# Twelve tiles of the last layer's first product as six pairs of seven quarter products, with sums on POOL

## The chip, the cores and the metric

The kernel runs on one core of one Trainium2 chip. The metric is the device time of one execution in microseconds (us); lower is better. Engines are named as the profile names them: PE (TensorE matmul), PEld (its weight load), DVE (VectorE), ACT (ScalarE), POOL (GpSimd), SP (SyncE, whose queue issues most DMAs).

## What is computed

Four residual layers over one sequence of S = 2048 tokens with D = 640 channels: twice (spectral filter, then token-mixing MLP). Cut to what matters here:

```python
def _B_ref(x, w1, b1, w2, b2):
    h = _layernorm(x, axis=-1)                  # (B, S, D)
    u = jnp.einsum("bsd,sf->bdf", h, w1) + b1   # (B, D, F), F = 1728
    u = _gelu(u)                                # tanh form
    y = jnp.einsum("bdf,fs->bds", u, w2) + b2
    return transpose(y)                         # (B, S, D)

x = x + _A_ref(_layernorm(x), A_w_r, A_w_i)     # 2-D FFT, filter, inverse FFT
x = x + _B_ref(_layernorm(x), ...)
x = x + _A_ref(_layernorm(x), ...)
x = x + _B_ref(_layernorm(x), ...)              # the last layer
```

Weights are float32. To keep that precision, the kernel splits each matmul operand into a float16 high part and a float16 low part and adds three products: high·high, high·low, low·high.

## The kernel before

The program is one class with a method for each stage. `run` (line 1411) does the opening stage, then for each of two rounds `a1` (428, filter), `a2` (696, inverse transform, residual and layernorm into `hf`), and the MLP: `b1st` (864) in the first round, `b2nd` (1112) in the second. The change is in `b2nd`, with small parts in `setup`, `a1` and `a2`. Nearly all instructions go through one helper (line 59, `Pin`), so the profile's line says little, and groups are told apart by tile names. While `self.pin` is set, each engine issues its instructions in the order in which the program text makes them.

**First product of the last layer, before.** The 1728 rows of w1's output are 14 tiles of 128 (the last tile holds 64 rows twice, with high parts in one half and low parts in the other; `dup`). The contraction over 2048 tokens is 16 slices j. `h` is kept as `hh[j]` (high) and `hl[j]` (low), each 128 x 2 x 320 (two halves of the channels); its float32 source `hf[j]` is released once `hl` is formed (pop at 1136). A tile takes 16 slices x 3 products x 2 halves = 96 matmuls of 128 x 128 by 320 columns; the dup tile takes 64. The order of tiles is `SEQ` (line 30): 0, 7, 6, 13, 1, 8, ...: a tile and its partner seven further on. The first two tiles go through `both_high` (1093), which multiplies by `hh` while `hl` is still being formed, and then through `rest`.

For each tile of weights: `wload` (828) brings two raw pieces of 128 x 1024 float32 over SP's queue; `wsplit` (840) has ACT write the scaled high part (`wh`) and DVE write raw·s − high (`wl`). After a tile's matmuls, ACT evicts it twice (value and square), DVE and ACT form the gelu in four steps (`q`, tanh, `f`), and `usplit` (1208) forms the operands of the second product: the quarters B11, B21, B22 and the sums T1 to T4 of quarters (`usums`, 1103, on DVE), each as a high part (ACT) and a low part (DVE).

**Second product, before.** It already takes pairs of output tiles d by seven products of quarters in place of eight: A11·B11, S1·T1, S2·T2, S3·T3, A12·B21, S4·B22, A22·T4, where S are sums of weight quarters formed by DVE (`form`, 1164), split by `hi` (ACT, 1181) and `lo` (DVE, 1188), and evictions add the products together. POOL does nothing in either product of this layer.

Of the kernel before, what the change touches and what calls it, by code (L numbers as in the profile page):

```python
# [29 lines left out]
SEQ = [t + 7 * i for t in (0, 6, 1, 2, 3, 4, 5) for i in range(2)]  # L30
# [36 lines left out]
class Layers:  # L67
# [41 lines left out]
    def setup(self):  # L109
# [17 lines left out]
        self.s2, self.c2 = (base.tile([128, NQ], F32, name=f"{a}p") for a in "sc")  # L127
        self.second, self.nr = False, 3
# [299 lines left out]
    def a1(self, first):  # L428
# [4 lines left out]
        self.hh = {j: ph.tile([128, 2, 320], F16, name=f"hh{j}_{self.n}") for j in HA}  # L433
# [262 lines left out]
    def a2(self, li):  # L696
# [4 lines left out]
        self.wp[1] = self.push("wb", side=self.sp)  # L701
        ph = self.push("hf", side=self.sp)
        self.hf = [ph.tile([128, 2, 320], F32, name=f"hf{j}_{self.n}") for j in range(NJ)]
# [399 lines left out]
    def usums(self, f, fs, *names):  # L1103

        B11, B12, B21, B22 = (f[:, i] for i in range(4))
        T1, T2, T3, T4 = (fs[:, i] for i in range(4))
        q = {"T1": (T1, B12, B11), "T2": (T2, B22, T1), "T3": (T3, B22, B12), "T4": (T4, B21, T2)}
        for n in names:
            a, b, c = q[n]
            self.V.tensor_tensor(a, b, c, op=ALU.subtract)  # L1110

    def b2nd(self, li):
# [6 lines left out]
        V, T = self.V, self.T  # L1119
        mm = self.PE.matmul  # L1120
        ADD, SUB, MUL = ALU.add, ALU.subtract, ALU.mult
        ph = self.push("h", side=self.sq)
        for j in range(NJ):
            if j not in HA:
                self.hh[j] = ph.tile([128, 2, 320], F16, name=f"hh{j}_{self.n}")
                T.activation(self.hh[j], self.hf[j], AF.Copy)
        self.pin = True
        self.wsplit(1, hi=False)
        self.h = []
        for j in range(NJ):  # L1130
            self.h.append((self.hh[j], ph.tile([128, 2, 320], F16, name=f"hl{j}_{self.n}")))
            V.tensor_tensor(self.h[j][1], self.hf[j], self.hh[j], op=SUB)
        V.tensor_tensor(self.s2, self.st[1][:, :NQ], self.st[1][:, NQ:], op=ALU.min)
        V.tensor_tensor(self.c2, self.ct[1][:, :NQ], self.ct[1][:, NQ:], op=ALU.max)
        self.pin = False
        self.pop("hf")
        self.nr = 4
        self.wr[1:] = (self.push(a, side=self.sp) for a in ("wr", "wr2", "wr3"))
        px = self.push("px", side=self.sp)
        pu = self.push("u", side=self.sp)  # L1140

        u = [pu.tile([128, 2, 7, 320], F16, name=f"u{f}_{self.n}") for f in range(7)]
        p = self.push("b1", side=self.sq)
        for m in (2, 3, 4, 5):
            self.wload(m)

        def ahead(m):

            self.wload(m + 4)
            if m + 1 < NFT:  # L1150
                self.wopen(m + 1)


        PQ = ("A11", "B11"), ("S1", "T1"), ("S2", "T2"), ("S3", "T3"), ("A12", "B21"), ("S4", "B22"), ("A22", "T4")
        UB = {a: i for i, a in enumerate(("B11", "B21", "B22", "T1", "T2", "T3", "T4"))}
        ops = [(d, *q) for d in range(NQ) for q in PQ]
        NP = len(ops)
        places = [(px, f"wo{i}") for i in range(3)] + [(q, a) for q in self.wp for a in ("wh", "wl")]
        src, wo = {}, {}

        def raw(d, a):
            return self.wraws[NFT + 2 * d + int(a[1]) - 1][int(a[2]) - 1]

        def form(n):

            if n >= NP:
                return
            d, a, _ = ops[n]
            if a[0] == "A":
                src[n] = raw(d, a)  # L1170
                return
            s = src[n] = self.t(px, [128, 7, 128], F32, a, 1)
            x, y, op = {
                "S1": ((d, "A21"), (d, "A22"), ADD), "S2": (n - 1, (d, "A11"), SUB),
                "S3": ((d, "A11"), (d, "A21"), SUB), "S4": ((d, "A12"), n - 3, SUB),
            }[a]
            x, y = (src[q] if isinstance(q, int) else raw(*q) for q in (x, y))
            V.tensor_tensor(s, x, y, op=op)

        def hi(n):  # L1180
            if n >= NP:
                return
            q, tag = places[n % 7]
            w = self.t(q, [128, NJ, 128], F16, tag, 1).rearrange("p (a b) c -> p a b c", a=2)[:, :, :7]
            wo[n] = w
            T.activation(w[:, 0], src[n], AF.Identity, scale=self.s2[:, ops[n][0]:][:, :1])

        def lo(n):
            if n >= NP:
                return  # L1190
            w = wo[n]
            V.scalar_tensor_tensor(w[:, 1], src[n], self.s2[:, ops[n][0]:][:, :1], w[:, 0], op0=MUL, op1=SUB)

        def prep(m):

            for c in range(2):
                if m + 1 < NFT:
                    self.wsplit(m + 1, (c,))
                yield
# [5 lines left out]
        def uhi(t, i, n, f):  # L1205
            T.activation(u[t][:, 0, i:i + n], f, AF.Identity, scale=self.su)

        def usplit(t, k, f, fs):
            if not k:
                uhi(t, 0, 1, f[:, 0:1])  # L1210
                ulo(t, 0, 1, f[:, 0:1])
                self.usums(f, fs, "T1")
                uhi(t, 3, 1, fs[:, 0:1])
                ulo(t, 3, 1, fs[:, 0:1])
            else:
                uhi(t, 1, 2, f[:, 2:])
                self.usums(f, fs, "T2", "T3", "T4")
                ulo(t, 1, 2, f[:, 2:])
                uhi(t, 4, 3, fs[:, 1:])
                ulo(t, 4, 3, fs[:, 1:])  # L1220

        def prod(ps, w, j, h, start=False, stop=False):
            for a in range(2):
                mm(ps[:, a, :320], w[:, j], h[:, a], start=start, stop=stop)

        dup = lambda m: SEQ[m] == NFT - 1

        def rest(m, ps, w):
            for j in range(NJ):
                yield j  # L1230
                prod(ps, w[0], j, self.h[j][1], stop=j == NJ - 1)

        def both(m, ps, w):
            for j in range(NJ):
                yield j
                prod(ps, w[0], j, self.h[j][0], start=j == 0)
                prod(ps, w[0], j, self.h[j][1], stop=dup(m) and j == NJ - 1)
                if not dup(m):
                    prod(ps, w[1], j, self.h[j][0], stop=j == NJ - 1)


        w = self.w.pop(0), self.w.pop(1)
        pss = self.big(), self.big()
        self.both_high(pss, w, prod)
        gc, gs = 1.0 / GC, GS * GC
        later = []
        for m in range(NFT):
            t, k = SEQ[m] % 7, SEQ[m] // 7
            if m < 2:
                ps, run = pss[m], rest(m, pss[m], w[m])  # L1250
                if m:
                    self.wopen(2)
            else:
                ps = self.big()
                run = both(m, ps, self.w.pop(m))
                ahead(m)
            steps = prep(m)
            for j in run:
                if m and j in ((1, 2) if m == 1 else (6, 8) if m == 2 else (2, 4)):
                    next(steps)  # L1260
                if j == 10:
                    for a in later:
                        a()
                    later = []
                if m == NFT - 2 and j == 8:
                    form(1)
                if m == NFT - 1 and j in (1, 4, 7, 10):
                    n = j // 3
                    if n != 1:
                        form(n)  # L1270
                    hi(n)
                    lo(n)
            pv, bb, c1 = ps[:, :, :320], self.b1[:, SEQ[m]:SEQ[m] + 1], self.ct[0][:, SEQ[m]:SEQ[m] + 1]
            if dup(m):

                sw = self.t(p, [128, 2, 320], F32, "sw", 1)
                T.activation(sw[:64], pv[64:], AF.Copy)
                T.activation(sw[64:], pv[:64], AF.Copy)
                V.tensor_tensor(sw, pv, sw, op=ADD)
                pv = sw  # L1280
            if not k:
                f = self.t(p, [128, 4, 320], F32, "f", 2)
                fs = self.t(p, [128, 4, 320], F32, "fs", 1)
            x = f[:, 2 * k:2 * k + 2]
            q = self.t(p, [128, 2, 320], F32, "q", 2)
            if m < NFT - 1:
                T.activation(x, pv, AF.Identity, scale=c1, bias=bb)
# [95 lines left out]
        for n in range(NP + 1):  # L1383
# [11 lines left out]
            if n:  # L1395
                hi(n + 3)
            if n > 1:
                lo(n + 2)
# [303 lines left out]
```

## Time and profile before

| | |
|---|---|
| runs shown | 1030.52 us median of 3 (1027.93 to 1032.33) |
| profiled execution, own time | 1028.95 us |
| its span | 1027.2 us |
| PE / PEld busy | 986.3 / 735.7 us (96% / 72%) |
| DVE / ACT / POOL busy | 725.5 / 571.2 / 265.7 us |
| granted TensorE clock, mean | 0.98 |

The span runs from the first to the last instruction; 1.75 us of the execution lie outside it. Matmuls are pipelined, so one matmul's recorded 299 ns is longer than the distance from one to the next; a few matmul records are missing. "Releaser" is the engine whose event ended a wait. The chain of waits follows the work that ended last, in order of time.

### The profile page before, as it was taken

Reading aid. Unit: us, or ns where it says so; the run is one execution under the profiler, and the core shown is the slowest. Engines: PE = TensorE matmul, PEld = TensorE weight load, DVE = VectorE, ACT = ScalarE, POOL = GpSimd, SP = SyncE. Lnnn points to the kernel's source line nnn. Section 1 sums busy time; section 2 is a strip of 40 time slices with the busy share of each in tenths; the row PEclk is TensorE's granted clock in tenths of the full one; section 3 lists DMA queues with packets and bytes.
Section 4 is the critical chain, followed back from the end, with each engine's and each line's share of the span. In section 5 each row is a group of like instructions: output and inputs, shape, how many; then the busy total and the mean of one; then the engine's idle time right before and its main releaser. Section 6 shows DMA issues by size and latency. Waiting matters only on the chain.

```text
span 1027.2 us, 20943 instructions
## 1 busy us (share of the span) xinstructions
PE 986.3 (96%) x8379; PEld 735.7 (72%) x8379; DVE 725.5 (71%) x1422; ACT 571.2 (56%) x874; POOL 265.7 (26%) x438
## 2 busy tenths in 40 slices
PE   4889999999999999999998999999999999999998
PEld 3768777677777777777776787776777777777776
DVE  7968978954333956666666797897655564988885
ACT  5847768675554556555542575774544454544541
POOL 6927857500000002222222675780000000000000
PEclk9589999999999999999999999999999999999999
DMA  7855356522222264444312644756322232445511
GB/s 230 277 173 168 116 167 222 207 83 99 77 77 74 72 233 155 138 135 123 124 55 86 214 125 130 223 177 210 108 82 83 72 109 77 141 154 175 164 44 52
DMA packets 55738, 139.48 MB, mean 136 GB/s; under 512 B 6461, under 2 KB 12249, under 8 KB 55641
## 3 DMA queue, kind: packets, MB, share of 16 engines
q1 hardware_dynamic: 54200, 131.97, 40.1%
q0 software_dynamic: 1440, 6.17, 2.0%
q8 instruction: 66, 1.08, 0.4%
q14 instruction: 32, 0.25, 0.1%
HBM read 115.05 MB, written 23.07 MB: 134 GB/s over the span
## 4 chain that ended last, share of the span: by engine, by line
PE 76%; DVE 13%; POOL 3%; issue 3%; DMA 2%; ACT 2%; SPq 0%; POOLq 0%; DVEq 0%; ACTq 0%
PE ps L59 76%; DVE st L59 2%; POOL xt L59 2%; DVE xt L59 2%; DVE f L59 1%; DVE Yl L59 1%; DVE s1l L59 1%; DVE hl L59 1%; DVE ta L59 1%; ACT eh L59 1%; DVE el L59 1%; DMA rest<-s1l 1%; POOL r L59 1%; DVE tb L59 1%; DMA stk<-rest 1%
## 5 line engine op out<-in xcount | busy, mean ns | idle before, releaser
L59 PEld LDWEIGHTS <-wh 128*128 128x128 f16 x2992 | 289.7, 98 | 113.4 <-issue 1.8
L59 PEld LDWEIGHTS <-wl 128*128 128x128 f16 x1616 | 157.9, 98 | 62.2 <-DVE wl L59 0.9
L59 PE MATMUL ps<-hh,wh 128*128 128x320 f16 x896 | 186.6, 299 | 0.7 <-ACT hh L59 0.7
L59 PE MATMUL ps<-hl,wh 128*128 128x320 f16 x896 | 184.7, 299 | 0.0
L59 PE MATMUL ps<-hh,wl 128*128 128x320 f16 x832 | 171.4, 299 | 0.6 <-DVE wl L59 0.6
L59 DVE SCALAR_TENSOR_TENSOR wl<-raw,s,wh 128x1024 f16<-128x1024 f32 (+2 forms) x88 | 105.4, 1202 | 87.4 <-ACT wh L59 87.3
L59 PE MATMUL ps<-uh,wl 128*128 128x320 f16 x448 | 133.1, 299 | 0.0
L59 PE MATMUL ps<-ul,wh 128*128 128x320 f16 x448 | 133.1, 299 | 0.0
L59 ACT ACTIVATE wh<-raw,s 128x1024 f16<-128x1024 f32 (+2 forms) x92 | 94.7, 1047 | 68.4 <-PE ps L59 61.6
L59 PE MATMUL ps<-uh,wh 128*128 128x320 f16 x416 | 124.3, 299 | 0.0
L59 ACT ACTIVATE junk<-raw 128x896 bf16<-128x896 f32 (+1 forms) x60 | 59.6, 994 | 46.5 <-DMA raw<-w 46.4
L59 POOL TENSOR_TENSOR r<-v,mh 128x1 f32<-128x1 f32 x64 | 37.4, 584 | 132.2 <-DVE nm L59 122.6
L59 PE MATMUL ps<-tDi,Yh 128*128 128x322 f16 x320 | 71.3, 300 | 0.2
L59 PE MATMUL ps<-u,wo 128*128 128x320 f16 x504 | 69.9, 299 | 0.0
L59 DVE TENSOR_TENSOR f<-eo 128x256 f32<-128x256 f32 (+1 forms) x124 | 39.1, 368 | 38.8 <-POOL eo L59 38.1
L59 PEld LDWEIGHTS <-wo 128*128 128x128 f16 x504 | 49.3, 98 | 19.1
L59 POOL TENSOR_TENSOR xt<-xt,ec 128x320 f32<-128x320 f32 x64 | 52.4, 841 | 32.8 <-DVE xt L59 32.6
L59 PE MATMUL ps<-ph,tS 128*128 128x321 f16 (+2 forms) x288 | 59.6, 289 | 1.3 <-DVE tb L59 1.3
L59 ACT ACTIVATE z<-xt,nb,r 128x640 f32<-128x640 f32 x31 | 28.5, 919 | 55.8 <-POOL z L59 43.5
L59 DVE BATCH_NORM_STATS2 st<-xt 128x6 f32<-128x320 f32 x126 | 55.3, 481 | 5.7 <-DMA xt<-x 4.6
L59 PE MATMUL ps<-tM,f 128*128 128x128 f32 x160 | 39.5, 426 | 19.8 <-DVE f L59 19.8
L59 POOL TENSOR_TENSOR eo<-z 128x320 f32<-128x320 f32 x62 | 53.3, 880 | 17.1 <-ACT z L59 15.1
(174 smaller groups left out, 1877.0 us busy)
## 6 DMA issues: line engine op xcount, KB each, us to landing
raw<-w SPq DMA_DIRECT2D x56, 512.0 KB
xt<-x SPq DMA_DIRECT2D x79, 320.0 KB
w<-w SPq DMA_DIRECT2D x48, 321.0 KB
x<-xt SPq DMA_DIRECT2D x47, 320.0 KB
raw<-w SPq DMA_DIRECT2D x32, 448.0 KB
raw<-w2z SPq DMA_DIRECT2D x32, 448.0 KB
out<-xt SPq DMA_DIRECT2D x15, 320.0 KB
tIM<-tIM POOLq DMA_DIRECT2D x8, 512.0 KB, 5.6
```

Of the source, the lines that this page charges most:

```text
L59: i = f(*a, **k)
```

## The change

The last layer's first product now computes only tiles 6 and 13 whole (`SEQ = [6, 13]`). The other twelve tiles are six pairs (d, d + 7), d = 0 to 5. Each pair is four quarters of weights (two tiles x two halves of the contraction) by four quarters of `h` (two halves of the contraction x two halves of the channels), taken by the same seven products as the second product. A product is 8 slices x 3 matmuls = 24 matmuls of 320 columns, 168 for a pair.

- The sums of weights S1 to S4 (128 x 1024 float32) are formed on POOL, S2, S3, S4 in place of raw quarters. DVE still forms them in the second product, except S1, S2, S3 of its first pair, which POOL forms.
- The sums of h, T1 to T4, are formed on POOL in place in `hf`'s rows (`tsum`: two instructions of 128 x 1280 each), then split by ACT (`thi`) and DVE (`tlo`). So `hf` stays until then, as one tile `hfa`; `hh` for j < 8 becomes one tile `hha`.
- Evictions put the seven products together: ACT and DVE read the product from PSUM, POOL adds pieces already in SBUF. The T sums of `u` (`usum`) move from DVE to POOL, except for the last pair.
- Raw quarters come through a ring of six buffers (`pump`), split weights through five places (`places`).
- At the start, work on tiles 6 and 13 is interleaved with the first sums; the seven products of pairs 0, 1 and 2 are interleaved as `FIRST` says; at the end, the last pair is finished in pieces (`half`, `split1`).

The diff, cut to its core:

```diff
-SEQ = [t + 7 * i for t in (0, 6, 1, 2, 3, 4, 5) for i in range(2)]
+SEQ = [6, 13]
...
-        self.hh = {j: ph.tile([128, 2, 320], F16, name=f"hh{j}_{self.n}") for j in HA}
+        self.hha = ph.tile([128, 8, 2, 320], F16, name=f"hha{self.n}")
+        self.hh = {j: self.hha[:, j] for j in HA}
...
-        self.hf = [ph.tile([128, 2, 320], F32, name=f"hf{j}_{self.n}") for j in range(NJ)]
+        self.hfa = ph.tile([128, NJ, 2, 320], F32, name=f"hf{self.n}")
+        self.hf = [self.hfa[:, j] for j in range(NJ)]
...
+        FIRST = "A11.0 A12.0 S1.0 S2.0 A11.1 A12.1 S3.0 S4.0 A22.0 S1.1 S2.1 A11.2 S3.1 S4.1 A22.1 S1.2 S2.2 A12.2 S3.2 S4.2 A22.2"
+        ops = [(int(q[-1]), q[:-2], P1[q[:-2]]) for q in FIRST.split()]
+        ops += [(d, *q) for d in range(3, ND) for q in P1.items()]
...
+        places = [(self.wp[0], "wl"), (self.wp[1], "wl"), (px, "wo"), (self.wp[0], "wh"), (self.wp[1], "wh")]
...
+        def form(n, W=V, p=None):
...
+            W.tensor_tensor(s, x, y, op=op)
...
+        def tsum(a, c, W=G):
+            j, k = slice(4 * c, 4 * c + 4), slice(8 + 4 * c, 12 + 4 * c)
+            B11, B12, B21, B22 = hfa[:, j, 0], hfa[:, j, 1], hfa[:, k, 0], hfa[:, k, 1]
+            o, x, y = {"T1": (B12, B12, B11), "T2": (B22, B22, B12), "T3": (B11, B22, B11), "T4": (B21, B21, B22)}[a]
+            W.tensor_tensor(o, x, y, op=SUB)
...
+        def tlo(a):
+            for c in range(2):
+                j = slice(4 * c, 4 * c + 4)
+                V.tensor_tensor(TT[a][1][:, j], tsrc(a, c), TT[a][0][:, j], op=SUB)
...
+        def product(n):
...
+            for j in range(8):
+                self.mm3(o, (w[:, 0, j], w[:, 1, j]), operand(b, j), j == 0, j == 7)
...
+            if a == "S2":
+                vs[d] = self.t(p, [128, 320], F32, "v", 1)
+                add(vs[d], ms[d])
+                G.tensor_tensor(f[:, 1], f[:, 1], vs[d], op=ADD)
+            if a == "A12":
+                act(0, bias=b0)
+                G.tensor_tensor(f[:, 0], f[:, 0], ms[d], op=ADD)
+            if a == "S3":
+                add(vs[d], vs[d])
+                (V if end else G).tensor_tensor(f[:, 3], f[:, 3], vs[d], op=ADD)
...
+            elif a == "A22":
+                act(2, bias=b1)
+                G.tensor_tensor(f[:, 2], f[:, 2], vs[d], op=ADD)
...
+        for d in range(3, ND):
+            b = at[d, "A11"]
+            forms.update({(d, "S1"): b - 5, (d, "S3"): b - 3, (d, "S2"): b - 2, (d, "S4"): b + 1})
+        for (d, a), n in sorted(forms.items(), key=lambda q: q[1]):
+            mid[n].append(lam(form, at[d, a], G))
+        for a, n in (("S1", N1 - 4), ("S3", N1 - 3), ("S2", N1 - 2)):
+            mid[n].append(lam(form, at2[0, a], G))
...
+        form(at[0, "S1"], G)
+        hlow(0)
+        hlow(1)
+        hi(0)
+        lo(0)
+        tsum("T1", 0)
+        tsum("T1", 1)
+        hlow(2)
+        hlow(3)
+        hi(1)
+        for i, w in enumerate((wh0, wh1)):
+            prod(pss[i], w, hlows, low)
+        product(0)
+        for i, w in enumerate((wh0, wh1)):
+            prod(pss[i], w, hlows, high, stop=True)
+        thi("T1")
+        hi(2)
+        tlo("T1")
+        lo(2)
+        lo(1)
+        form(at[0, "S3"], G)
+        tsum("T2", 0)
+        tsum("T2", 1)
+        form(at[0, "S2"], G)
...
+        product(1)
...
+        for n in range(2, N1):
+            product(n)
+            for e in first[n]:
+                e()
+            for e in mid[n]:
+                e()
+            hi(n + 3)
+            lo(n + 3)
+            for e in last[n]:
+                e()
+            pump()
```

`first[n]` holds the evictions of product n − 1, `mid[n]` the sums of weights (and T3, T4 at n = 2), `last[n]` the gelu steps and the splits of `u`. `N1` is 42.

More of the change, by code (lines that the diff above doesn't have):

```diff
@@ L127, in setup @@
         self.s2, self.c2 = (base.tile([128, NQ], F32, name=f"{a}p") for a in "sc")
+        self.s1p, self.c1p = (base.tile([128, 7], F32, name=f"{a}p1") for a in "sc")
         self.second, self.nr = False, 3
@@ L1120, in b2nd @@
         mm = self.PE.matmul
         ADD, SUB, MUL = ALU.add, ALU.subtract, ALU.mult
+        self.wr[1] = self.push("wr", side=self.sq)
+        px = self.push("px", side=self.sq)
         ph = self.push("h", side=self.sq)
[L1123 to L1154, printed above, removed]
@@ L1155, in b2nd @@
-        UB = {a: i for i, a in enumerate(("B11", "B21", "B22", "T1", "T2", "T3", "T4"))}
-        ops = [(d, *q) for d in range(NQ) for q in PQ]
-        NP = len(ops)
-        places = [(px, f"wo{i}") for i in range(3)] + [(q, a) for q in self.wp for a in ("wh", "wl")]
+        pt = self.push("T", side=self.sq)
+        hx = self.push("hx", side=self.sq)
+        hha, hfa, hf = self.hha, self.hfa, self.hf
+        hhb, hlb = (ph.tile([128, 8, 2, 320], F16, name=f"{a}b{self.n}") for a in ("hh", "hl"))
@@ new lines, in b2nd, with pump @@
+        order = []
+        for d in range(ND):
+            names = ("A11", "A21", "A12", "A22"), ("A11", "A12", "A21", "A22"), ("A11", "A22", "A21", "A12")
+            order += [(1, d, a) for a in (names[d] if d < 3 else ("A21", "A22", "A11", "A12"))]
+        order += [(2, d, a) for d in range(NQ) for a in ("A21", "A22", "A11", "A12")]
+        pieces, need = {}, {}
+        def pump():
+            while len(pieces) < len(order):
+                k = len(pieces)
+                if k >= 6 and need[order[k - 6]]:
+                    return
+                f, d, a = order[k]
+                r, c = int(a[1]) - 1, int(a[2]) - 1
+                pool, n = (self.wr[0], 2) if k % 6 > 3 else (self.wr[1], 4)
+                raw = self.t(pool, [128, 8, 128], F32, "raw", n)
+                src, q = (A["w1"][d + 7 * r], 8) if f == 1 else (A["w2z"][d + NQ * r], 7)
+                pieces[f, d, a] = raw[:, :q]
+                nc.sync.dma_start(raw[:, :q], src[:, c * q:c * q + q])
+                place = f == 1 or d == 0
+                need[f, d, a] = {
+                    "A11": {"S2"} if place else {"A11", "S2f", "S3f"}, "A21": {"S3"} if place else {"S1f", "S3f"},
+                    "A12": {"S4"} if f == 1 else {"A12", "S4f"}, "A22": {"A22"},
+                }[a]
@@ L1182, in hi @@
                 return
[L1183 to L1186, printed above, removed]
+            if ops[n][1][0] == "A" and n not in src:
+                form(n)
+            q, tag = places[n % 5]
+            w, k = self.t(q, [128, NJ, 128], F16, tag, 1), 8 if n < N1 else 7
+            w = wo[n] = w[:, :2 * k].rearrange("p (a b) c -> p a b c", a=2)
+            T.activation(w[:, 0], src[n], AF.Identity, scale=scale(n))
         def lo(n):
@@ new lines, in hlow @@
+        def hlow(c):
+            j = slice(4 * c % 8, 4 * c % 8 + 4)
+            if c < 2:
+                V.tensor_tensor(hl0[:, j], hfa[:, j, 0], hha[:, j, 0], op=SUB)
+                V.tensor_tensor(hl1[:, j], hfa[:, j, 1], hha[:, j, 1], op=SUB)
+            else:
+                V.tensor_tensor(hlb[:, j], hfa[:, 4 * c:4 * c + 4], hhb[:, j], op=SUB)
+        hhigh = lambda j, a: hha[:, j, a] if j < 8 else hhb[:, j - 8, a]
+        hlows = lambda j, a: (hl1 if a else hl0)[:, j] if j < 8 else hlb[:, j - 8, a]
@@ new lines, in prod, with operand @@
+        def prod(ps, w, h, js, start=False, stop=False):
+            for j in js:
+                for a in range(2):
+                    mm(ps[:, a, :320], w[:, j], h(j, a), start=start and j == 0, stop=stop and j == NJ - 1)
+        def operand(b, j):
+            if b == "B11":
+                return hha[:, j, 0], hl0[:, j]
+            if b[0] == "B":
+                return tuple(q[:, j, int(b[2]) - 1] for q in (hhb, hlb))
+            return tuple(q[:, j] for q in TT[b])
+        bank = {}
@@ L1226, in b2nd @@
[L1226 to L1239, printed above, removed]
@@ L1242, in b2nd @@
-        w = self.w.pop(0), self.w.pop(1)
-        pss = self.big(), self.big()
[L1244 to L1287, printed above, removed]
-                T.activation(q, pv, AF.Square, scale=c1, bias=bb)
-                V.scalar_tensor_tensor(q, q, gc, x, op0=ADD, op1=MUL)
-                T.activation(q, q, AF.Tanh, scale=gs)
-                V.scalar_tensor_tensor(x, q, 1.0, x, op0=ADD, op1=MUL)
-                later.append(lambda t=t, k=k, f=f, fs=fs: usplit(t, k, f, fs))
@@ new lines, in b2nd @@
+        early, late, low, high = range(NJ - 4), range(NJ - 4, NJ), range(8), range(8, NJ)
+        for js in (early, late):
+            prod(pss[0], wh0, hhigh, js, start=True)
+            prod(pss[0], wl0, hhigh, js)
+            prod(pss[1], wh1, hhigh, js, start=True)
+        form(at[0, "S1"], G)
[10 more added lines that the diff above has]
+            prod(pss[i], w, hlows, low)
@@ new lines, in b2nd @@
+        product(0)
[10 more added lines that the diff above has]
+        form(at[0, "S2"], G)
+        self.pop("hx")
+        p = self.push("b1", side=self.sq)
+        pr = self.push("br", side=self.sp)
+        f = pr.tile([128, 4, 320], F32, name=f"fr{self.n}")
+        q0, q1 = (pr.tile([128, 2, 320], F32, name=f"qr{k}{self.n}") for k in range(2))
@@ new lines, in b2nd, with uopen @@
+        last[4] += [g0(1), g0(2), dup1, g0(3), g1(1)]
+        last[5] += [g1(2), lam(thi, "T4"), lam(tlo, "T4"), g1(3)]
+        def uopen():
+            self.pop("br")
+            self.pop("hf")
+            pu = self.push("u", side=self.sp)
+            u.update({t: pu.tile([128, 2, 7, 320], F16, name=f"u{t}_{self.n}") for t in range(7) if t != t0})
+        u = {t0: self.u6}
+        for k in range(3):
+            last[7 + k].append(lambda k=k: usplit(k, t0, f))
+        last[10] = [uopen] + last[10]
@@ new lines, in b2nd, with half, go, split1 @@
+        D5 = ND - 1
+        q5 = {}
+        def half(i, *ks):
+            def go():
+                if i // 2 not in q5:
+                    q5[i // 2] = self.t(p, [128, 2, 320], F32, "q", 2)
+                for k in ks:
+                    gelu(k, fs[D5][:, i:i + 1], q5[i // 2][:, i % 2:i % 2 + 1])
+            return go
+        def split1(i, n, x):
+            return [lambda: uhi(D5, i, n, fs[D5][:, x:x + n]), lambda: ulo(D5, i, n, fs[D5][:, x:x + n])]
+        last[N1 - 3] += [half(0, 0, 1)]
```

247 lines of the change are left out of this document (180 added, 67 removed).

## The prediction

> **What bounds the kernel now.** I read the chain of waits first, then busy times by stretch, then groups by tile and shape, then single instructions in order of time.
>
> ```profile
> 692.29 11.04 DVE hl L59 x15
> ...
> 712.13 311.52 PE ps L59 x2292
> ```
>
> In the chain of waits (start, us, what), from 712 us to the end it is one piece of PE work; just before it DVE forms `hl`. 311.52 / 2292 = 0.1359 us is the distance between matmuls.
>
> ```profile
> 683.18 0.99 PE L59 MATMUL ps<-hh,wh 128*128 128x320 f16 x6
> 695.34 0.43 PE L59 MATMUL ps<-hh,wh 128*128 128x320 f16 x2 [0.19 <-ACT hh L59]
> 863.73 8.31 PE L59 MATMUL ps<-u,wo 128*128 128x320 f16 x60
> ...
> 740.00:760.00 20.00, 20.00 (x150) 14.42 (x148) 9.84 (x14) 7.98 (x10) 0.00 (x0) 1.00 0.29 88
> 875.00:1012.00 137.00, 137.00 (x1011) 98.65 (x1009) 117.26 (x141) 62.75 (x71) 0.00 (x0) 1.00 0.41 132
> ```
>
> In order of time (start, us), the first product runs from 683.2 to 863.7. The stretch rows (PE, PEld, DVE, ACT, POOL busy, granted clock, DMA) show PE full at clock 1.00, DVE at about half in the first product and 86% in the second, and POOL at nothing. So PE binds both, and matmuls taken out shorten the kernel only if the work put in stays beside PE.
>
> **The change part by part.** *Matmuls removed:* a pair takes 168 for 192; 6 x 24 = 144 fewer, x 0.1359 = 19.6 us. That leaves 96 + 64 + 42 x 24 = 1168. The 96 by `hh` end as now at about 698.6 (24 late ones after 695.34). The other 1072 are 145.7 us, so PE alone would reach the second product at 844.
>
> *What goes beside it* must be priced by instruction.
>
> ```profile
> L59 DVE SCALAR_TENSOR_TENSOR wl<-raw,s,wh 128x1024 f16<-128x1024 f32 x24 | 30.7, 1284 | 44.4 <-ACT wh L59 44.4
> L59 DVE TENSOR_TENSOR hl<-hf,hh 128x640 f16<-128x640 f32 x16 | 11.8, 820 | 0.0
> L59 DVE SCALAR_TENSOR_TENSOR wh<-raw,s,wl 128x512 f16<-128x512 f32 x2 | 1.5, 752 | 0.0
> L59 ACT ACTIVATE wh<-raw,s 128x1024 f16<-128x1024 f32 x24 | 27.4, 1143 | 40.3 <-PE ps L59 35.0 <-issue 5.2
> L59 ACT ACTIVATE q<-ps,b1s,c 128x640 f32<-128x640 f32 x12 | 10.5, 873 | 0.0
> L59 ACT ACTIVATE u<-fs,su 128x960 f16<-128x960 f32 x6 | 6.6, 1096 | 4.0 <-DVE fs L59 4.0
> L59 DVE SCALAR_TENSOR_TENSOR u<-ps,cp,m 128x320 f32<-128x320 f32 x8 | 4.4, 551 | 4.7 <-PE ps L59 4.7
> ...
> L59 POOL TENSOR_TENSOR xl<-ta,xh 128x642 f16<-128x642 f32 x30 | 42.9, 1434 | 22.2 <-ACT xh L59 22.2
> L59 POOL TENSOR_TENSOR ta<-ta,tb 128x256 f32<-128x256 f32 x2 | 1.3, 632 | 0.0
> L59 POOL TENSOR_TENSOR xl<-ta,xh 128x130 f16<-128x130 f32 x2 | 0.9, 441 | 0.0
> L59 POOL TENSOR_TENSOR ta<-tb,ta 128x65 f32<-128x65 f32 x2 | 0.6, 298 | 0.0
> L59 POOL TENSOR_TENSOR eo<-z 128x320 f32<-128x320 f32 x62 | 53.3, 880 | 17.1 <-ACT z L59 15.1 <-DVE f L59 1.8 <-ACT v L59 0.2
> ```
>
> These are groups by shape (busy us, mean ns of one). DVE: (1284 − 752) / 512 = 1.04 ns an element. POOL has no sum of 1024 or 1280 in the trace. Below: 0.298 for 65 and 0.75 for 321 (next fence) give 1.75 ns an element, so 1.97 us for 1024 and 2.42 for 1280. Above: 880 / 320 with nothing fixed, 2.75 ns, so 2.8 and 3.5 us. The nearest by type and contiguity is the first (plain float32 rows); I take it and keep the other for the range.
>
> The decisive question is whether POOL and DVE run side by side. This trace answers it in the filter stage, where the same DVE instruction (`wl<-raw,s,wh`) meets POOL's sums:
>
> ```profile
> 602.82 1.33 DVE L59 SCALAR_TENSOR_TENSOR wl<-raw,s,wh 128x512 f16<-128x512 f32 x1
> 605.00 0.87 DVE L59 SCALAR_TENSOR_TENSOR ta<-ps,sx,w 128x642 f32<-128x642 f32 x1
> 607.32 0.74 DVE L59 SCALAR_TENSOR_TENSOR wl<-raw,s,wh 128x512 f16<-128x512 f32 x1
> 611.23 0.96 DVE L59 SCALAR_TENSOR_TENSOR wl<-raw,s,wh 128x512 f16<-128x512 f32 x1
> 627.84 0.91 DVE L59 TENSOR_TENSOR ta<-ta,tb 128x65 f32<-128x65 f32 x1
> ...
> 602.84 0.75 POOL L59 TENSOR_TENSOR ta<-tb,ta 128x321 f32<-128x321 f32 x1
> 604.77 1.42 POOL L59 TENSOR_TENSOR xl<-ta,xh 128x642 f16<-128x642 f32 x1 [1.18 <-ACT xh L59]
> 607.46 1.21 POOL L59 TENSOR_TENSOR ta<-tb,ta 128x321 f32<-128x321 f32 x1
> 610.89 0.75 POOL L59 TENSOR_TENSOR ta<-ta,tb 128x321 f32<-128x321 f32 x1
> 611.60 1.21 POOL L59 TENSOR_TENSOR ta<-tb,ta 128x321 f32<-128x321 f32 x1
> 627.26 1.41 POOL L59 TENSOR_TENSOR xl<-ta,xh 128x642 f16<-128x642 f32 x1 [0.26 <-ACT xh L59]
> ```
>
> They do not. At 602.82 DVE's 512 elements take 1.33 us in place of 0.74: POOL's sum runs to 603.59, and DVE ends 0.56 later, its 0.53 of elements. At 607.32 DVE is first and POOL takes 1.21 in place of 0.75, ending 0.61 after DVE. At 611.23 they alternate: POOL ends 611.64, DVE 0.55 later, POOL's next 0.62 later. At 627.84 DVE needs 0.91 us for 65 elements, until POOL's 1.41 us end. At 605.00, with one operand in PSUM, DVE is not slowed beside POOL. So two-operand SBUF work of DVE and POOL's sums take turns, whole instruction by whole instruction; one holds the turn for its elements (DVE n x 1.04 ns + 0.02; POOL its duration − 0.14), and the rest can overlap.
>
> The Trainium skill, "SBUF — State Buffer", section "Who interferes with whom", has the same rule without a limit of length: a port pair is held for the whole instruction. The longest case here is 642 elements; if the page did not hold for 1024 and more, the last rival below would be the sum.
>
> *Turn-taking work of the new stage.* POOL: 24 sums of 1024 x 1.83 = 44.0; three of 896 for the second product x 1.61 = 4.8; 46 of 320 (4 evictions and 4 T sums in each of five pairs, 2 evictions in the last pair, 4 T sums for tile 6 and 13's rows) x 0.61 = 28.1; eight T sums of h of 1280 x 2.28 = 18.3. Together 95.2 us. DVE: 42 `lo` x 1.08 = 45.4; three of 896 x 0.95 = 2.8; 28 gelu steps of 640 x 0.68 = 19.0; low parts of u, 7 x 2240 elements in three instructions = 16.6; eight `tlo` of 1280 x 1.35 = 10.8; two `hlow` of 2560 = 5.4; four sums of the last pair = 1.4. Together 101.4. Sum 196.6; some 3 us (the last pair's `u`) come after PE has gone on. So 193.7 us of turns against 145.7 of PE: **the shared turn becomes the bound**. For one middle pair it is 12.2 (POOL) + 12.7 (DVE) = 24.9 against 22.8 on PE now and 26.1 before; the T sums, their splits and tile 6 and 13's gelu come on top.
>
> *When it starts.* POOL's first sum needs raw pieces that SP can request only behind its stores of x.
>
> ```profile
> 686.92 1.64 POOL L59 TENSOR_TENSOR xt<-xt,ec 128x320 f32<-128x320 f32 x2
> 691.13 26.66 SPq L834 DMA_DIRECT2D raw<-w  x12
> 692.21 11.85 DVE L59 TENSOR_TENSOR hl<-hf,hh 128x640 f16<-128x640 f32 x16
> 705.00:720.00 15.00, 14.39 (x107) 10.09 (x105) 10.00 (x15) 11.15 (x16) 0.00 (x0) 1.00 0.92 321
> ```
>
> The last x store waits for POOL until 688.6. Four pieces of 0.524 MB at the 321 GB/s of 705 to 720 take 6.5 us, with a landing delay 697.5. By then DVE has done tile 13's split and the first half of `hl` (1.2 + half of 11.85), so turn-taking begins at 697.5.
>
> *Sum.* With no slack, 697.5 + 193.7 = 891.2 against 863.7: +27.5. With no overlap of what is fixed in each instruction (11.85 / 16 = 0.74 a step for 640 on DVE, so 112 us; 0.71 a step for 321 on POOL, so 103; less 3), 212 us, +45.8. Both engines often queue, but they also wait for ACT, PE and each other: I take the middle, +36.7. 1028.95 + 36.7 = **1065.7 us**, made against the profiled execution, which lies 1.6 under the median of the runs.
>
> *Where PE feels it first.* `lo(1)` stands on DVE behind `hlow`, `tlo` of T1 and `lo(2)`, each taking turns with S1, T1, S3 and T2 on POOL: seven DVE pieces (11.3 us) and six POOL turns (12.8 us) from 697.5 reach 721.6. PE would be ready for product 1 about 712, so some 9 us of idle there; the rest comes spread over the 42 products. Behind DVE's `lo` stand the evictions, the gelu and later `lo`; ACT's squares wait for POOL's additions, and `hi` of later products behind them. The lead of three products (9.8 us) smooths this but adds no turns.
>
> *Costed at nothing.* ACT: 7 x 1.14 for high parts, 4 x 0.87 for the gelu, 2240 elements of u at 1.1 us for 960, five evictions of 320 at about 0.5: some 17 us a pair, under 22.8. Single-operand evictions (3 x 0.55 a pair) run beside POOL; uncovered, they cost 9.9 us in all. Tile 13 in place of tile 7 gives ACT 0.6 us more and DVE 1.1 less at the end of `a2`. `hfa` and `hha` as one tile: the first layer's loads are early. Six raw buffers: 24 pieces in place of 28 whole-tile halves, DMA at 0.29. Second product: the same sums on DVE, five places with PE four products behind; its 163.5 us stand. The handover (T1 of the last pair, late on a crowded DVE): 0 to 3 us, taken as 0.
>
> The Trainium skill, "GPSIMD Engine Reference", section "Performance versus the Vector engine", gives about 2.6 cycles an element at 1.2 GHz for a two-input sum, 2.2 ns. The trace's plain rows give 1.75; by the page POOL's 52,200 elements would cost 22 us more and the time would be about 1088.
>
> **The rivals.**
> 1. *POOL is slower on long or strided rows.* T sums read runs of 320 out of 640, as `eo` does; the `eo` and `xl` rows speak for it, the plain rows against. From `xl` (0.44 for 130, 1.43 for 642: 1.9 ns) to `eo` (2.75): 8 to 52 us more. With 22, 1088.
> 2. *POOL is quicker on long sums.* At 1.4 ns an element 18 us go: 1048. Against: 65, 256 and 321 lie on one line.
> 3. *PE stays the bound; faster.* Place: DVE's `lo` and POOL's sums in the same step. If DVE's work fell into POOL's idle times or long sums could be shared, the three-product lead would hide it; price: only about 2 us of start, 1028.95 − 19.6 + 2 = 1011. It decides from the point where 48 us of the turns (193.7 − 145.7) vanish; no loss is left from 28 us. Against: POOL's 95 us and DVE's 101 cannot both find idle time in 146.
>
> **How the numbers follow.** Forecast (1056 to 1075) 0.58; rival 1 0.22; rival 2, with all between 1036 and 1056, 0.12; rival 3 0.06; about unchanged 0.02. Likeliest 1065.7. The range leaves out rival 3, half of rival 1's upper end and the lowest part of rival 2: 1044 to 1092. Under 0.5% (5 us) a measurement of this kernel cannot be told from no change; so faster 0.06, same 0.03, slower 0.91.
>
> **What would show it.** Right: in the new stage POOL's sums of 1024 and DVE's `lo` last longer on average than 1.97 and 1.28 us, ending just after one another; PE idles some 50 to 65 us there, waiting for DVE's low parts; product 1 starts near 721; the second product starts near 890 to 910 and still takes 163.5 us. Wrong: DVE's `lo` keeps 1.28 us while POOL runs, or PE shows no idle beyond 10 us. If POOL's shortest 1024 is over 2.2 us, rival 1; under 1.5, rival 2.

## The result and the profile after

The changed kernel takes 1100.84 us (median of 4 runs, 1098.87 to 1101.68) against 1029.99 us for the kernel before (4 runs): a ratio of 1.068, interval 1.066 to 1.071. Its profiled execution takes 1100.38 us with a span of 1098.6 us, 71.4 us more than the span before. The forecast was 1065.7 us, range 1044 to 1092: the direction came true, and the time lies above the range.

The busy times of the page of the changed kernel:

```profile
PE 990.0 (90%) x8235; PEld 725.9 (66%) x8235; DVE 818.9 (75%) x1430; ACT 603.0 (55%) x914; POOL 432.5 (39%) x519
```

From its chain of waits (start, us, what); before, all from 712 us on was one piece of PE:

```profile
843.28 2.97 DVE f L59
...
849.51 4.36 POOL f L59 x3
...
861.65 2.31 POOL raw L59
...
874.97 2.97 DVE f L59
...
946.82 148.25 PE ps L59 x1090
```

DVE and POOL, with pieces of ACT between them, carry most of the chain through the first product, and PE carries it only from 946.8 on. One pair repeats after 874.97 − 843.28 = 31.7 us; on PE a pair is 22.8 us.

Busy times by stretch (PE, PEld, DVE, ACT, POOL, granted clock, DMA):

```profile
705.00:720.00 15.00, 9.41 (x55) 5.94 (x56) 15.00 (x5) 4.82 (x6) 15.00 (x4) 0.77 0.01 1
740.00:760.00 20.00, 12.87 (x93) 8.81 (x91) 18.81 (x9) 7.10 (x9) 17.47 (x6) 1.00 0.24 80
842.00:874.00 32.00, 27.69 (x187) 18.49 (x186) 23.24 (x18) 15.31 (x20) 21.20 (x14) 0.95 0.21 66
945.00:1083.00 138.00, 137.32 (x1012) 98.71 (x1010) 118.72 (x142) 64.70 (x72) 0.00 (x0) 1.00 0.43 142
```

Where PE was full before (150 matmuls in 740 to 760), it now issues 93, while DVE and POOL are both nearly always "busy", DVE with 9 instructions in 18.8 us. In the later pairs (842 to 874) neither is full. There ACT stands between them and waits for POOL's results; from its waits between 690 and 916 (total us, times, longest):

```profile
ACT wl L59 <- POOL raw L59: 23.6, 5, 8.7
ACT u L59 <- POOL f L59: 19.2, 4, 8.3
```

From 945 on all is as before.

Two of DVE's groups, then three of POOL's by tile (duration min/median/max in ns): sums of 320 in the evictions, the T sums of 1280 and sums of weights:

```profile
L59 DVE SCALAR_TENSOR_TENSOR wl<-raw,sp,wl 128x1024 f16<-128x1024 f32 x16 | 32.0, 2001 | 11.6 <-ACT wl L59 11.5
L59 DVE TENSOR_TENSOR hlb<-hf,hhb 128x2560 f16<-128x2560 f32 x2 | 10.4, 5239 | 0.0
```

```profile
L59 POOL TENSOR_TENSOR f<-f,v x16: 859/1790/1841, 752.7 to 912.4; 128x320 f32<-128x320 f32 x16
L59 POOL TENSOR_TENSOR hf<-hf x8: 2900/4134/5457, 699.8 to 748.6; 128x1280 f32<-128x1280 f32 x8
L59 POOL TENSOR_TENSOR raw<-S,raw x7: 2339/2350/3582, 722.1 to 920.8; 128x1024 f32<-128x1024 f32 x6, 128x896 f32<-128x896 f32 x1
```

The same `lo` of 1024 elements that took 1284 ns now takes 2001 on average in this group of 16, and a `hlow` of 2560 takes 5.24 us where the prediction counted 2.7. POOL's shortest times in these rows are 859, 2339 and 2900 ns for 320, 1024 and 1280 elements: (2339 − 859) / 704 = 2.10 ns an element, not 1.75. The Trainium skill, "GPSIMD Engine Reference", section "Performance versus the Vector engine", states about 2.6 cycles an element for a two-input sum, which at 1.2 GHz makes an estimate of 2.2 ns; these rows lie nearer to it than to the 1.75 that the prediction took from the filter stage.

One stretch of single instructions shows the turns at full length:

```profile
808.42 2.36 POOL L59 TENSOR_TENSOR raw<-raw,raw 128x1024 f32<-128x1024 f32 x1
808.55 2.92 DVE L59 SCALAR_TENSOR_TENSOR f<-q,f 128x640 f32<-128x640 f32 x1 [0.81 <-ACT q L59]
810.74 2.93 POOL L59 TENSOR_TENSOR S<-raw,raw 128x1024 f32<-128x1024 f32 x1
811.39 3.36 DVE L59 SCALAR_TENSOR_TENSOR wh<-raw,sp,wh 128x1024 f16<-128x1024 f32 x1
```

POOL's sum ends at 810.78; DVE's gelu step, issued beside it, ends 0.69 later, its own 640 elements. POOL's next sum ends 2.20 after that, and DVE's `lo` 1.08 after that. Each waits for the whole of the other's instruction, at 1024 elements as at 65.

Last, the order of time on PE: the start of the first product, then the handover to the second product:

```profile
710.50 1.63 PE L59 MATMUL ps<-hlb,wh 128*128 128x320 f16 x8 [2.27 <-DVE hlb L59]
...
728.04 0.71 PE L59 MATMUL ps<-hhb,wl 128*128 128x320 f16 x2 [7.68 <-DVE wl L59]
...
916.29 2.61 PE L59 MATMUL ps<-u,wo 128*128 128x320 f16 x18
928.61 0.43 PE L59 MATMUL ps<-u,wo 128*128 128x320 f16 x1 [9.71 <-ACT u L59]
...
929.68 4.28 PE L59 MATMUL ps<-u,wh 128*128 128x320 f16 x18
936.21 0.30 PE L59 MATMUL ps<-u,wh 128*128 128x320 f16 x1 [2.25 <-ACT u L59]
```

The second product starts at 916.3 in place of 863.7: +52.6. From there to the end it takes 1098.6 − 916.3 = 182.3 us in place of 163.5: +18.8, lost between 918.9 and 946.8 in gaps and in matmuls at a lower clock (4.28 us for 18 in place of 2.61). Together 71.4. Below, "handover" is always the span less the second product's start less 163.5.

### The profile page after: what moved, and what is told of

It is laid out like the page before. It is cut to its first block, busy times and chain, and to the rows that moved or that the text cites. A ratio compares the mean times of both kernels' runs of the same rounds, so it can differ in the third digit from the quotient of the medians.

```text
span 1098.6 us, 20851 instructions
## 1 busy us (share of the span) xinstructions
PE 990.0 (90%) x8235; PEld 725.9 (66%) x8235; DVE 818.9 (75%) x1430; ACT 603.0 (55%) x914; POOL 432.5 (39%) x519
## 4 chain that ended last, share of the span: by engine, by line
PE 55%; DVE 20%; POOL 10%; issue 6%; ACT 6%; DMA 2%; SPq 0%; POOLq 0%; DVEq 0%; ACTq 0%
PE ps L59 55%; POOL f L59 4%; DVE f L59 3%; POOL raw L59 2%; DVE wl L59 2%; DVE st L59 2%; DVE hl L59 2%; POOL xt L59 2%; DVE xt L59 1%; DVE Yl L59 1%; DMA raw<-w 1%; DVE s1l L59 1%; DVE ta L59 1%; DVE hlb L59 1%; ACT eh L59 1%
## 5 line engine op out<-in xcount | busy, mean ns | idle before, releaser
L59 PEld LDWEIGHTS <-wh 128*128 128x128 f16 x2734 | 267.8, 99 | 145.5 <-issue 16.6
L59 PEld LDWEIGHTS <-wl 128*128 128x128 f16 x1790 | 175.8, 99 | 97.9 <-DVE wl L59 20.1
L59 DVE SCALAR_TENSOR_TENSOR wl<-raw,s,wh 128x896 f16<-128x896 f32 (+2 forms) x64 | 74.6, 1170 | 43.3 <-ACT wh L59 43.3
L59 PE MATMUL ps<-hl,wh 128*128 128x320 f16 x496 | 101.8, 299 | 0.1
L59 ACT ACTIVATE wh<-raw,s 128x896 f16<-128x896 f32 (+2 forms) x68 | 67.4, 1013 | 27.8 <-PE ps L59 26.3
L59 PE MATMUL ps<-u,wh 128*128 128x320 f16 x462 | 68.1, 308 | 2.9 <-ACT u L59 2.2
L59 DVE TENSOR_TENSOR f<-eo 128x256 f32<-128x256 f32 (+1 forms) x124 | 39.1, 368 | 38.7 <-POOL eo L59 38.1
L59 PE MATMUL ps<-u,wl 128*128 128x320 f16 x462 | 65.1, 299 | 1.6 <-DVE wl L59 1.4
L59 PEld LDWEIGHTS <-wo 128*128 128x128 f16 x444 | 43.0, 98 | 32.7 <-issue 10.4
L59 PE MATMUL ps<-hha,wl 128*128 128x320 f16 x288 | 59.0, 299 | 0.9 <-DVE wl L59 0.9
L59 PE MATMUL ps<-hha,wh 128*128 128x320 f16 x288 | 58.1, 299 | 1.3 <-ACT wh L59 1.3
```

The lines of the kernel that those rows point to most:

```text
L59: i = f(*a, **k)
```

## The experiments

My theory: DVE's work on two SBUF operands and POOL's sums take turns, instruction by instruction, which fills the first product; the handover is in part the last pair's own chain of gelu and `u`. The rivals: PE or DMA is late for another reason, POOL is simply slow and PE waits for its results, or DVE has too much work of its own. Each run below is a single execution, beside executions of the kernel before at 1029 to 1031 us; the four runs of the changed kernel spread over 2.8 us.

**Sums back to DVE, group by group.** Four kernels move POOL's sums of the changed kernel to DVE: the weights' sums alone, all, the sums of 320 alone, the T sums of h alone.

```diff
-            mid[n].append(lam(form, at[d, a], G))
+            mid[n].append(lam(form, at[d, a], V))
...
-        def usum(f, a, W=G, o=None):
+        def usum(f, a, W=V, o=None):
...
-                G.tensor_tensor(f[:, 1], f[:, 1], vs[d], op=ADD)
+                V.tensor_tensor(f[:, 1], f[:, 1], vs[d], op=ADD)
...
-        def tsum(a, c, W=G):
+        def tsum(a, c, W=V):
```

Weights' sums:

> The changed kernel with the weights' sums (24 of 1024 and three of 896) on DVE; the T sums of h, the additions and the T sums of u stay on POOL. Turn-taking theory, with POOL at the 2.1 ns an element that the changed kernel's shortest sums show (2.34 us for 1024, 0.86 for 320): turns fall from 212 us to about 182 (POOL 55, DVE 130, less 3), the second product starts near 885, the time is about 1060 to 1070 us, and DVE's low parts of 1024 last 1.3 to 1.6 us on average against 1.9. Rival (DVE and POOL run freely side by side, POOL is only late): low parts last 1.28 us with or without the change, DVE gets 29 us more, and the time falls by less than 15 us.

All:

> The changed kernel with all of POOL's sums of this stage on DVE, so that POOL does nothing there, as before the change. Turn-taking theory: DVE does each sum in half of the time that POOL would have held the turn; DVE's steps add up to about 184 us from 699, the second product starts near 880, time about 1045 to 1060 us. Rival (free side by side): DVE gets 66 us more of work and loses nothing by POOL, so the time rises above 1100.

Sums of 320:

> The changed kernel with only the 46 small sums of 320 (additions of products and T sums of u) on DVE; weights' sums and T sums of h stay on POOL. Turn-taking theory: turns fall by 46 x (0.72 - 0.35) = 17 us, and the waits of ACT for POOL's small sums go, so the handover shortens too: 1065 to 1080 us. If the handover (18.8 us) does not come from POOL's small sums, only the 17 us are seen: about 1083.

T sums of h:

> The changed kernel with only the eight T sums of h (1280 each) on DVE. Turn-taking theory: eight turns of 2.76 become eight of 1.35, 11 us fewer, all of it at the start: about 1087 to 1091 us, and the first product of the first pair behind the low parts (A12) starts some 8 us earlier than 728. Rival (free side by side): DVE gets 11 us more at a place where it binds, so the time does not fall.

| on DVE | time, us | second product starts | handover | span against the changed kernel |
|---|---|---|---|---|
| none (the changed kernel) | 1100.38 | 916.3 | 18.8 | |
| weights' sums | 1077.17 | 897.9 | 14.0 | −23.2 |
| sums of 320 | 1087.75 | 909.9 | 12.5 | −12.7 |
| T sums of h | 1090.91 | 906.8 | 18.8 | −9.5 |
| all | 1057.09 | 879.3 | 12.5 | −43.3 |

The weights' sums alone and the sums of 320 alone gain less than expected; the other two lie within what was expected (with the T sums of h on DVE the first pair's A12 starts at 721.5, 6.5 us earlier, where some 8 were expected). With POOL out of the stage, `lo` is back at the time that it had before the change:

```profile
L59 DVE SCALAR_TENSOR_TENSOR wl<-raw,sp,wl 128x1024 f16<-128x1024 f32 x16 | 20.3, 1276 | 0.2 <-ACT wl L59 0.2
```

The gains of the three parts add up (45.4 against 43.3), and per element they are alike: 23.2 / 27264, 12.7 / 14720 and 9.5 / 10240 are 0.85, 0.86 and 0.93 ns. That is most of the difference between POOL's 2.10 and DVE's 1.04 ns. Under turns an element costs its time on whichever engine has it, so moving it to the faster one gains the difference. A chain in which ACT waits for POOL's results, one after another, would gain by the same difference; these four runs do not tell the two apart. And 28 us remain in the last row (span 1055.3 against 1027.2). Its stretch:

```profile
800.00:840.00 40.00, 35.84 (x258) 24.58 (x257) 38.53 (x50) 22.82 (x28) 0.00 (x0) 1.00 0.20 69
```

Without POOL, DVE alone is the bound (38.5 of 40 us), and PE issues 258 matmuls where 40 us hold 294. Neither DVE alone nor DVE with POOL has room for the sums; ACT, busy for 22.8 of the 40 us, was not tried.

**POOL's sums in the kernel before.** To the kernel before, 48 sums of 1024 on POOL are added, two at each split of weights, that read raw pieces and write a scratch tile which nothing reads. In a second kernel the same 48 places write only (fills of 1536).

```diff
+        psc = self.push("scr", side=self.sp)
+        scr = psc.tile([128, 1536], F32, name="scr")
...
+                    for _ in range(2):
+                        ra, rb = self.wraws[m + 1]
+                        G.tensor_tensor(scr[:, :1024].rearrange("p (a b) -> p a b", a=8), ra, rb, op=ADD)
```

Sums:

> The kernel before, with 48 more sums on POOL in the first product: four for each of twelve tiles, each adding the two raw pieces of the tile (128 x 1024 float32) into a scratch tile that nobody reads. Nothing waits for them but the raw buffers. Turn-taking theory: DVE's low parts of 1024 go from 1.28 us to 1.7 to 2.2 on average and POOL's sums from 2.34 us upwards; the time stays within 5 us, since DVE had half of its time free there. Rival (free side by side): low parts stay at 1.28.

Fills:

> As the run with 48 more sums, but each sum is a fill of 128 x 1536 float32 with zero into the scratch tile: POOL is busy but reads nothing. If the turn is one for reading, low parts stay at 1.28 us; if any work of POOL takes the turn, they grow as they do beside sums (1.7 to 2.2 while POOL is busy). The time stays within 3 us either way.

Sums: 1068.73 us, +38.7, though nobody waits for a result of POOL; the second product starts at 903.5 and its handover is 0. I had expected the time unchanged and low parts of 1.7 to 2.2 us. The raw buffers stay in use longer, but the loads are not late by it: ACT waits for one once, 12.6 us against 12.2 in the kernel before. PE waits 18.8 us for DVE's low parts, where it waited 0.6. From the kernel with the sums, in order of time, then its groups and its stretch:

```profile
759.50 22.86 POOL L59 TENSOR_TENSOR scr<-raw,raw 128x1024 f32<-128x1024 f32 x8
760.03 3.37 DVE L59 SCALAR_TENSOR_TENSOR wl<-raw,s,wh 128x1024 f16<-128x1024 f32 x1
...
768.78 2.65 DVE L59 SCALAR_TENSOR_TENSOR u<-f,su,u 128x320 f16<-128x320 f32 x1
...
773.90 0.81 DVE L59 TENSOR_TENSOR sw<-ps,sw 128x640 f32<-128x640 f32 x1
```

```profile
L59 DVE SCALAR_TENSOR_TENSOR wl<-raw,s,wh 128x1024 f16<-128x1024 f32 x22 | 60.9, 2769 | 1.1 <-ACT wh L59 1.1
```

```profile
740.00:780.00 40.00, 23.08 (x133) 14.21 (x132) 39.93 (x16) 12.72 (x15) 38.90 (x15) 0.76 0.11 39
```

While POOL has sums in its queue, each DVE instruction with two SBUF operands costs one of POOL's on top of its own time: 3.37 us for 1024 elements (2.2 + 1.1), 2.65 for 320. The one with an operand in PSUM keeps 0.81. DVE does 16 instructions in 39.9 us, and PE falls to 133 matmuls. DVE was about half busy in this stretch before, so I had thought that it would have room; it had none, because the price is per instruction.

Fills: 1034.41 us, a little more than the 3 us that were allowed for. Its groups:

```profile
L59 DVE SCALAR_TENSOR_TENSOR wl<-raw,s,wh 128x1024 f16<-128x1024 f32 x24 | 30.7, 1283 | 45.0 <-ACT wh L59 45.0
L59 POOL MEMSET scr<- 128x1536 f32 x45 | 62.1, 1379 | 2.4
```

DVE keeps 1283 ns beside 62 us of POOL: it is reading that takes turns, not POOL being busy. (The 4 us more come at the start: the fills stand in POOL's queue ahead of its last work on x, and the second product starts at 869.2.) The Trainium skill, "SBUF — State Buffer", section "Who interferes with whom", says so: a DVE instruction with two SBUF inputs contends with a GpSimd instruction that reads SBUF, not with one that only writes. These two runs agree.

**Fills in place of the weights' sums in the changed kernel.** The first product's 24 sums of weights become two fills each, 950 ns apiece, so POOL's own work stays nearly as long (1.9 us for 2.34) and the reads go. The waits for the raw pieces go with them. The weights' sums are left out of the computation.

```diff
-            W.tensor_tensor(s, x, y, op=op)
+            if f == 1:
+                G.memset(s, 0.0)
+                G.memset(s, 0.0)
+            else:
+                W.tensor_tensor(s, x, y, op=op)
```

> The changed kernel with each of POOL's 24 sums of weights in the first product replaced by two fills of the same 128 x 1024 tile with zero, about as long as a sum, which read nothing; the weights' sums are left out of the computation. Turn-taking theory (reads): 24 turns of 2.2 us go, 53 us; the second product starts at 870 to 890 and the time is 1050 to 1068 us, as quick as or quicker than with these sums on DVE (1077). Rival (POOL is only late, its own length counts): POOL is as long in its queue as before, and the time stays above 1090.

Measured: 1070.00 us; the second product starts at 886.2, 30.1 earlier, as expected; the handover stays 18.5, which I had not counted in, and the time lies 2 us above what was expected. Not all of the 30.1 us are the reads: the fills are 24 x 0.44 = 10.6 us shorter in all, and in the changed kernel POOL's sums wait 7.0 us for raw pieces. And POOL's results are still waited for: ACT waits 15.6 us for POOL before `wl` (23.6 in the changed kernel) and 18.6 us before `u` (19.2), and a pair still takes 25.8 us where PE alone needs 22.8. How much of the first product's loss is turns and how much is the wait for results that POOL makes late, no run separates.

**The handover.** Of the 18.8 us, 12.5 are left where POOL has no sums. A first guess was that the last pair's slice holds up the first four products of the second; so, with all sums on DVE, these four leave it to a later place and the weights behind them are split earlier.

```diff
-            late = n in (2, 3)
+            late = n < 4
...
-                for k in (2, 3):
+                for k in range(4):
...
-            for k in {0: (), 3: (), 4: (2, 3)}.get(n, (n - 1,)):
+            for k in {0: (), 1: (), 2: (), 3: (), 4: (0, 1, 2, 3)}.get(n, (n - 1,)):
```

> The variant with all sums on DVE, and the handover eased: the second product's first four products (not only the third and fourth) leave the last pair's slice for later, and the fourth product's weights are split before the last pair's gelu. If the handover's 12.5 us are PE waiting for the last pair's u behind a crowded DVE, PE has 72 matmuls (9.8 us) to do meanwhile in place of 18, and about 5 us are won: 1051 to 1053 us against 1057. If PE waits there for something else (weights, loads of x), the time stays at 1057.

A miss: 1060.48 us, handover 16.0. The gap moved; on PE:

```profile
904.32 5.37 PE L59 MATMUL ps<-u,wl 128*128 128x320 f16 x21 [6.77 <-DVE xt L59]
```

PE now waits for DVE to evict the four held-back products. So I took the two sources apart: only the sums at the end to DVE; and, with all sums on DVE, the last pair's gelu left out (its loop over steps made empty, the other steps deleted).

```diff
+            W = V if t == ND - 2 else G
-                usum(f, "T1")
+                usum(f, "T1", W)
...
-                G.tensor_tensor(f[:, 1], f[:, 1], vs[d], op=ADD)
+                (V if end else G).tensor_tensor(f[:, 1], f[:, 1], vs[d], op=ADD)
...
-            mid[n].append(lam(form, at2[0, a], G))
+            mid[n].append(lam(form, at2[0, a], V))
```

> The changed kernel, with only the end of the first product moved from POOL to DVE: the three first sums of the second product, the sums of u for the pair of the second product's quarters and the last pair's two additions. Theory (of the 18.8 us between the two products, 12.5 are the last pair's gelu and u on ACT and DVE and 6.3 are POOL's turns with DVE): the first product stays as long, the second product starts at 912 to 917 us, the 18.8 us become 12 to 14, and the time is 1091 to 1096 us. Rival (all of it is the sums' own work, on whichever engine): 18 to 20 us remain and the time is 1098 to 1103 us.

```diff
-                for k in ks:
+                for k in ():
...
-        gelu(0, f5[:, 2], q2)
...
-        gelu(1, f5[:, 2], q2)
-        gelu(2, f5[:, 2], q2)
...
-        gelu(3, f5[:, 2], q2)
```

> All sums on DVE, as in the run in which POOL has none (1057.1 us, 12.5 us between the products), and the last pair's gelu steps left out, so that its u is formed from the raw value. Theory (the 12.5 us are the chain of the last pair's gelu on ACT and DVE, which the second product must wait for): 6 to 8.5 us remain, and the time is 1050 to 1053 us. Rival (they are DVE's remaining queue of slices and sums): 11 to 13 us remain and the time is 1055 to 1058 us.

Measured: 1094.94 us, start 916.8, handover 12.9, within what was expected; and 1048.96 us, start 878.0, handover 5.7, a little better than expected. PE at the handover without the last gelu, and the same two waits with it (all sums on DVE):

```profile
881.84 0.30 PE L59 MATMUL ps<-u,wo 128*128 128x320 f16 x1 [1.28 <-ACT u L59]
...
886.80 0.30 PE L59 MATMUL ps<-u,wh 128*128 128x320 f16 x1 [0.89 <-ACT u L59]
887.72 2.88 PE L59 MATMUL ps<-u,wh 128*128 128x320 f16 x20 [0.62 <-DVE u L59]
```

```profile
885.31 0.30 PE L59 MATMUL ps<-u,wo 128*128 128x320 f16 x1 [3.40 <-ACT u L59]
...
892.91 0.43 PE L59 MATMUL ps<-u,wh 128*128 128x320 f16 x1 [2.62 <-ACT u L59]
893.83 5.49 PE L59 MATMUL ps<-u,wh 128*128 128x320 f16 x20 [0.49 <-DVE u L59]
```

So about 6 of the 18.8 us are POOL's sums at the end, 7 the last pair's gelu, and 6 are left, which no run took apart. Of the 7, part is PE's clock: with shorter gaps the same 20 matmuls take 2.88 us in place of 5.49 (granted clock 1.00 in 887.7 to 890.4, 0.50 in 893.8 to 899.1).

No run beats the kernel before; the best that computes everything is all sums on DVE, 1057.09 us. Fewer pairs with whole tiles behind them, which might shorten the handover, was not tried.

## Why the prediction was right and wrong

- *Matmuls removed (19.6 us).* Right as a count (8379 matmuls before, 8235 after), but without effect: PE is not what the first product waits for.
- *DVE and POOL take turns by whole instructions.* Right, and shown in the kernel before by unread sums (1.28 to 2.77 us for `lo`) against fills (1.28). The limit of length that I could not exclude does not exist at 1024 or 1280 elements. Rival 3 falls. That the turns alone bind is not shown: in the later pairs neither engine is full, and ACT waits for POOL's results.
- *POOL's price of 1.75 ns an element.* This is the step that failed first. It came from one family of sums, `ta` of 65 to 321 in the filter stage; here it is 2.10. Length is not the reason: a sum of 320 takes 859 ns here, one of 321 there 0.75 us. `eo` was the better row, and the prediction put it at the far end of the range by giving it no fixed time: its 880 ns less the fixed part of the `ta` rows (0.298 us less 65 x 1.75 ns, 0.18) make 2.2 ns. What sets the two families apart, no run shows. With turns of 2.20 for 1024, 1.93 for 896, 0.72 for 320 and 2.76 for 1280 (each shortest time less 0.14), POOL's 95.2 us become 113.8: **+18.6**. This is rival 1, whose sign (a shortest 1024 over 2.2 us) came true at 2.34; it had 0.22 and 1088 us.
- *The handover, "0 to 3 us, taken as 0".* **+18.8**, the other step that failed. The sentence looked at T1 alone. The chain behind it (last evictions, gelu, `u` on ACT and DVE, in PE's order ahead of everything else) has hardly any PE work beside it (18 matmuls, then a wait of 9.71 us for `u`): the last pair's quarters are finished by its fourth to seventh product, one after the other.
- *Slack, the middle of no slack and no overlap.* With the corrected rate no slack gives 697.5 + 113.8 + 101.4 − 3 = 909.7, and 916.3 was measured: 6.6 us of slack where the middle had 9.2, **−2.6**. What the 6.6 consist of was not taken apart; a pair's 31.7 us are 14.6 (POOL's turns) + 12.7 (DVE's) + 4.4.
- The sum: 36.7 + 18.6 + 18.8 − 2.6 = 71.5, measured 71.4. It closes because the slack is what the other terms leave; only the 18.6 and the 18.8 rest on rows of their own.
- *Product 1 at about 721.6.* 728.0; six POOL turns at the measured rate give 2.7 of the 6.4. *What is costed at nothing:* for the changed kernel it held in that the second product runs without a wait behind the handover (1090 matmuls in 148.25 us from 946.8 on, 0.136 each as before), but the run with all sums on DVE shows that DVE's own queue, one-operand evictions included, would bind next (38.5 of 40 us).
- *The range.* Its upper end took in rival 1 at 22 us and not the handover; the two misses have one sign and were priced apart.

## What to carry to other kernels

An idle POOL is no free adder beside a busy DVE: while POOL has sums in its queue, each of DVE's instructions with two SBUF operands can wait out one whole POOL instruction, so count DVE's instructions, not only its busy share. Price POOL from more than one family of rows: sums of 320 or 321 took 0.75 to 0.88 us in one trace. Seven products of quarters that save matmuls also finish their four results only by the fourth to the last of them; look for what PE can do between the last product and its reader. Where an edit takes work from an engine that binds and gives it to ones that do not, add up their work in that stage first, shared turns included.

## What the runs showed that was not expected

The price of turns is per instruction: 48 sums that nothing reads cost 38.7 us, and a DVE instruction of 320 elements takes 2.65 us beside them. And a PE that has idled for some us can come back at half clock. PE at the handover of the kernel in which only the sums at the end are on DVE, then its stretch with the granted clock:

```profile
916.76 2.75 PE L59 MATMUL ps<-u,wo 128*128 128x320 f16 x18
923.19 0.43 PE L59 MATMUL ps<-u,wo 128*128 128x320 f16 x1 [3.69 <-ACT u L59]
923.78 0.69 PE L59 MATMUL ps<-u,wo 128*128 128x320 f16 x2 [0.16 <-DVE u L59]
924.26 5.01 PE L59 MATMUL ps<-u,wh 128*128 128x320 f16 x18
```

```profile
924.00:929.20 5.20, 5.20 (x20) 2.87 (x19) 4.59 (x10) 1.71 (x5) 0.00 (x0) 0.50 0.01 3
```

After 3.7 us of idle time, 18 matmuls take 5.01 us; less the last one's own 0.474 (the longest in this kernel's trace), 17 steps of 0.267 us each, half the rate of the 0.136 of the kernel before. Not each gap does this: behind one of 2.29 us at 750.1 in the changed kernel the matmuls follow at 0.136 us. But a gap of some us in a PE stream can cost more than its length, and a stage that waits often (granted clock 0.77 in 705 to 720 above) waits at a lower clock; how much of the first product's loss this is, no run separates.
